# The last block's first layer as seven half-size products per 2x2 blocking, in an attention-plus-FFN kernel

## The chip, the cores and the metric

The kernel runs on one core of one Trainium2 chip. The metric is device time in microseconds, the median of the runs; lower is better. All times below are microseconds unless marked ns. The engines are PE (TensorE, matrix multiplications), DVE (VectorE), ACT (ScalarE), POOL (GpSimd) and SP (SyncE, which here only issues DMAs).

## The reference

```
# q, k, v: 8 batches, 8 heads, 576 positions, 64 wide; window of 64 positions
scores = q @ k^T / 8, masked to 0 <= pos_q - pos_k < 64
attn   = softmax(scores) @ v                  # per batch and head
x      = attn, heads side by side             # 4608 tokens x 512
h      = relu(x @ w_in)                       # w_in 512 x 2048
out    = (h * h) @ w_out                      # w_out 2048 x 512, out 4608 x 512 float32
```

The two multiplications with `w_in` and `w_out` are called layer 1 and layer 2.

## The kernel before

The 4608 tokens are worked on in nine blocks of 512: blocks 0 to 7 are the first 512 positions of each batch, and block 8 (called `B`) holds the last 64 positions of all eight. For each block there are the attention units (four pairs of heads: scores `Sc`, mask `M`, product with v `A`, transposition `X` into `xT`), layer 1 and layer 2.

*Layer 1* is `F1(g, f)`: for each of 16 slices of 128 of the 2048 hidden columns, four multiplications of 128x512 sum up in one PSUM bank (`hps`, L358). DVE takes the relu out of the bank (`hr`, L361), and ACT squares it into the 16-bit tile `h2` (L362). The banks of `hps` are two (`ps_f1`).

*Layer 2* of blocks 2 to 8 is already done with seven products in place of eight: `L2S(g, p, s, banks)` computes product p (1 to 7) of one half s of the token tiles, each as eight multiplications of 128x256 (`product`, L446). Two PSUM banks serve it, `chain` (256 columns of one bank) and `side` (two halves, `pa` and `pb`). For one s the products go in the order 1, 2, 6, 5, 7, 3, 4: products 1, 6, 7 and 4 add to one another in `chain`, and between them ACT copies the partial result out, scaled (`scaled`, L460), or DVE adds it to what is there (`plus`, L463). Product 1 starts a new sum in `chain`, so it must come after the copy made for the product that was in `chain` before. The sums of blocks of h that the products need are made by `S_sum` (DVE, L422, `hsum`), the sums of blocks of `w_out` once by `T_sum` (`wsum`).

All instructions are put in order by hand. The last loop goes over n = 1 to 8; the pass n is called phase n here. In phase n the layer 2 of block n and the layer 1 of block n + 1 alternate on PE. A string `order` of the digits 1 and 2 says in which order the groups of layer 1 and 2 follow, one group per digit; `put(i, work)` places other work ahead of group i: the attention units of block n + 2, the S sums, and DMA loads. Phase 7 has 16 groups of layer 1 of block 8 and 14 products of block 7, and no attention work. Phase 8 has only the 14 products of block 8; there the two halves s have banks of their own (`more`, which are the two `ps_f1` banks, and `chain` with `side`).

Each engine runs its own list in program order. An instruction that waits holds up all that stand behind it on its engine. PE's order in phase 7 is layer 1, layer 2, layer 1, ... ; ACT's list holds the squares of layer 1 and the scaled copies of layer 2, DVE's the relus, the adds of layer 2 and the S sums.

The attention tiles `at_ps[0]` and `at_ps[1]` (two PSUM banks each) are free in phase 7, since no attention is left. The pool `tpool` (five tiles with the tag T) holds the transposed q and k; `stp` (ten 128x512 32-bit tiles) holds loaded inputs.

Of the kernel before, what the change touches and what calls it, by code (L numbers as in the profile page):

```python
# [8 lines left out]
FP32 = mybir.dt.float32  # L9
FP16 = mybir.dt.float16  # L10
AF = mybir.ActivationFunctionType
ALU = mybir.AluOpType
# [3 lines left out]
def kernel(  # L16
# [13 lines left out]
    nc = tc.nc  # L30
# [3 lines left out]
    P = 128  # L34
    HP = H // 2
    NBLK = B + 1
    DMC = DM // P
    FFC = DFF // P
# [6 lines left out]
    stp = ctx.enter_context(tc.tile_pool(name="stp", bufs=10))  # L45
    p16p = ctx.enter_context(tc.tile_pool(name="p16p", bufs=6))
    vpool = ctx.enter_context(tc.tile_pool(name="vpool", bufs=2))
    tpool = ctx.enter_context(tc.tile_pool(name="tpool", bufs=5))
    apool = ctx.enter_context(tc.tile_pool(name="apool", bufs=2))
    xtpool = ctx.enter_context(tc.tile_pool(name="xtpool", bufs=2))  # L50
    h2pool = ctx.enter_context(tc.tile_pool(name="h2pool", bufs=2))
# [3 lines left out]
    ps_f1 = ctx.enter_context(tc.tile_pool(name="ps_f1", bufs=2, space=bass.MemoryType.PSUM))  # L55
# [47 lines left out]
    st = {}  # L103
# [12 lines left out]
    def copy(engine, out, in_):  # L116
        if engine is nc.scalar:
            engine.activation(out=out, in_=in_, func=AF.Copy, scale=1.0)  # L118
        else:
            engine.tensor_copy(out=out, in_=in_)  # L120


    w_in_sb = const.tile([P, DMC, DFF], FP16, name="w_in_sb")
# [121 lines left out]
    pm, av, xs, xT = {}, {}, {}, {}  # L245
    at_ps = [ps_at.tile([P, 2, 512], FP32, name=f"at{i}") for i in range(2)]
# [84 lines left out]
    def X(g, hp, engine=nc.scalar, pool=ps_tr, tag="tr", own=None):  # L331

        if g not in xT:
            xT[g] = xtpool.tile([P, DMC, 512], FP16, name="xT", tag="xT")
        if g == B:
            nc.sync.dma_start_transpose(out=xT[g][:, hp, :].rearrange("p (j t) -> p j t", j=4),
                                        in_=xs[g, hp][:].rearrange("p j h d -> p (j h d)"))
            return
        if own is not None:
            tr = at_ps[own][:, 0, :].bitcast(FP16).rearrange("p (a b) -> p a b", a=2)  # L340
        else:
            tr = pool.tile([P, 2, 512], FP16, name="xtr", tag=tag)
        for jp in range(4):
            nc.tensor.transpose(out=tr[:, 0, jp * P:(jp + 1) * P], in_=xs[g, hp][:, jp, :, :],  # L344
                                identity=ident[:])
        copy(engine, xT[g][:, hp, :], tr[:, 0, :])


    h2 = {}

    def F1(g, f, pool=ps_f1, tag="f1", into=None):
        if g not in h2:
            h2[g] = h2pool.tile([P, FFC, 512], FP16, name="h2", tag="h2")
        hps, done = open_f1.pop((g, f), (None, 0))
        if hps is None:
            hps = into if into is not None else pool.tile([P, 512], FP32, name="hps", tag=tag)
        for c in range(done, DMC):
            nc.tensor.matmul(hps[:], w_in_sb[:, c, f * P:(f + 1) * P], xT[g][:, c, :],  # L358
                             start=(c == 0), stop=(c == DMC - 1))
        hr = opool.tile([P, 512], FP32, name="hr", tag="hr")  # L360
        nc.vector.tensor_scalar(out=hr[:], in0=hps[:], scalar1=0.0, scalar2=None, op0=ALU.max)  # L361
        nc.scalar.activation(out=h2[g][:, f, :], in_=hr[:], func=AF.Square)  # L362
# [41 lines left out]
    HF = FFC // 2  # L404
# [6 lines left out]
    def a_of(g, i, j, s):  # L411
        t0 = 256 * i + 128 * s
        return h2[g][:, j * HF:(j + 1) * HF, t0:t0 + 128]
# [4 lines left out]
    def s_of(k, s):  # L418
        return S_sb[:, k - 1, :, 128 * s:128 * s + 128]

    def minus(out, a, b, op=ALU.subtract, engine=None):
        (engine or nc.vector).tensor_tensor(out=out, in0=a, in1=b, op=op)  # L422
# [11 lines left out]
    def S_sum(g, k, s):  # L434
        if k == 1:
            minus(s_of(1, s), a_of(g, 1, 0, s), a_of(g, 1, 1, s), ALU.add)
        elif k == 2:
            minus(s_of(2, s), s_of(1, s), a_of(g, 0, 0, s))
        elif k == 3:
            minus(s_of(3, s), a_of(g, 0, 0, s), a_of(g, 1, 0, s))  # L440
        else:
            minus(s_of(4, s), a_of(g, 0, 1, s), s_of(2, s))

    def product(to, a, b, start):
        for f in range(HF):
            nc.tensor.matmul(to, a[:, f, :], b[:, f, :], start=start and f == 0, stop=f == HF - 1,  # L446
                             skip_group_check=True)

    def flush():
        while to_store:  # L450
            to_store.pop(0)()
# [61 lines left out]
    seq = list(range(NBLK))  # L513
# [3 lines left out]
    with tc.manual_schedule():  # L517
# [21 lines left out]
        dve, pool, act = nc.vector, nc.gpsimd, nc.scalar  # L539
# [60 lines left out]
        three = [in_f1, in_f1, in_f2]  # L600
# [60 lines left out]
        first = iter([lambda f=f: F1(g1, f, into=at_ps[1][:, 1, :] if f == 2 else None) for f in range(FFC)])  # L661
# [5 lines left out]
        def A(g, hp, i=1):  # L667
            AV(g, hp, i)
            N(g, hp)
# [36 lines left out]
        done = 12  # L706
        chain = ps_f2.tile([P, 512], FP32, name="chain", tag="f2")
        side = ps_tr.tile([P, 512], FP32, name="side", tag="tr")
        for n in range(1, NBLK):
            g = seq[n]  # L710
            last = n == NBLK - 1
            one = None if last else seq[n + 1]
            if n == 1:
                second = [lambda ts=ts, i=i: F2(g, ts, i, None, None, into=(chain, side)[ts % 2])
                          for ts in range(4) for i in range(4)]
            elif last:
                more = [ps_f1.tile([P, 512], FP32, name="more", tag="f1") for _ in range(2)]
                banks = [(more[0][:, 0:HC], more[1]), (chain[:, 0:HC], side)]
                second = [lambda p=p, s=s: L2S(g, p, s, banks[s])
                          for p, s in ((1, 0), (2, 0), (1, 1), (6, 0), (2, 1), (5, 0), (7, 0),  # L720
                                       (6, 1), (3, 0), (4, 0), (5, 1), (7, 1), (3, 1), (4, 1))]
            else:
                second = [lambda p=p, s=s: L2S(g, p, s, (chain[:, 0:HC], side))
                          for s in range(2) for p in ORDER]
            first = [] if last else [lambda f=f: F1(one, f) for f in range(FFC)]
            order = ("22222222" + 8 * "112" if n == 1 else
                     "2" * 14 if last else
                     ("2112121212121211" if n == 2 else "1212121212121211") + "21212121121122")
            a, b = iter(first), iter(second)
            fill = [next(a if c == "1" else b) for c in order]  # L730
            at = {}

            def put(i, *work):
                at.setdefault(i, []).extend(work)

            if n == 1:
                put(0, lambda: Sc(g2, 3), lambda: A(g2, 2))
                put(2, lambda: M(g2, 3))
                put(3, lambda: X(g2, 2, own=1))
                put(5, lambda: A(g2, 3))  # L740
                put(7, lambda: X(g2, 3, own=1))
                for i, k in ((1, 1), (3, 2), (6, 3), (8, 4)):
                    put(i, lambda k=k: T_sum(k))
            else:
                for i, k, s in (((0, 1, 1), (0, 2, 1), (2, 4, 0), (3, 3, 1), (4, 4, 1)) if last else
                                ((2, 4, 0), (4, 1, 1), (6, 2, 1), (9, 3, 1), (18, 4, 1))):
                    put(i, lambda k=k, s=s: S_sum(g, k, s))
            if not last:
                end = len(fill) - 1
                put(24 if n == 1 else 20, lambda: S_sum(one, 3, 0))  # L750
                put(end if n == 1 else end - 1, lambda: S_sum(one, 1, 0))
                put(end, lambda: S_sum(one, 2, 0))
            base = 4 * (n + 2)
            for i, two in zip((11, 22) if n == 1 else (9, 20) if n == 2 else (9, 17) if n == 6 else (8, 19),
                              (units[base:base + 2], units[base + 2:base + 4])):
                for t, u in enumerate(two):
                    if u is not None:
                        put(i, lambda u=u, t=t: Sc(*u, i=t))
                        put(i + 3 + t, lambda u=u: M(*u))
                        put(i + 6, lambda u=u, t=t: A(*u, i=t))  # L760
                        put(i + (7 if u[0] == B else 8 + t), lambda u=u, t=t: X(*u, own=t))
            for i, group in enumerate(fill):
                for work in at.pop(i, []):
                    work()
                total = 12 + (30 * (n - 1) + i + 1) * (len(load_list) - 12) // 140
                while done < total and (parts_left or pending):
                    next_part()
                    done += 1
                group()
            assert not at, at.keys()  # L770
# [30 lines left out]
```

## Time and profile before

| what | us |
|---|---|
| median of 3 runs (297.67 to 298.23) | 298.13 |
| the profiled execution | 298.21 |
| its span, first to last instruction | 296.2 |
| phase 6 (223.90 to 253.63) | 29.73 |
| phase 7 (253.63 to 279.67) | 26.04 |
| phase 8 with the last stores (279.67 to 296.20) | 16.53 |

A phase is counted here from the start of its first group on PE to that of the next phase's first. The page of the profile gives the busy time of each engine and the chain of work that ended last; the timeline gives instructions in order of time, where "x8" means eight that follow one another, the second column is their length together, and a bracket at the end names an idle time ahead of them and what ended it. Matmuls overlap, so a burst of eight is written with 1.04 although the next one starts 0.87 after it.

### The profile page before, as it was taken

What the parts mean: (1) busy time and instruction counts of PE and PEld (TensorE: products, weight loads), DVE (VectorE), ACT (ScalarE), POOL (GpSimd) and SP (SyncE); (2) the same over time, 40 slices, a digit from 0 to 9 for tenths busy, and PEclk for the clock granted to TensorE, in tenths of its full rate; (3) what the DMA queues carried; (4) which work ended last, traced back from release to release, by engine and by line L of the source; (5) the groups of instructions that cost most, each with busy time, mean ns of one, the idle gap of its engine ahead of it and who ended that gap; (6) DMA issues with size and microseconds to landing.
All of it is one profiled execution on the core that took longest, in us unless ns stands there. A gap on an engine that the chain in (4) does not pass through costs nothing.

```text
span 296.2 us, 7372 instructions
## 1 busy us (share of the span) xinstructions
PE 287.7 (97%) x2905; PEld 180.3 (61%) x2905; DVE 216.3 (73%) x379; ACT 170.3 (57%) x292; POOL 125.8 (42%) x215
## 2 busy tenths in 40 slices
PE   7899999999999999999999999999999999999994
PEld 5543545555445466667666766676667666766783
DVE  4677539588867787878778877987788679866651
ACT  3666757688366656565665566556655654444521
POOL 4668848984383267229425633913232000000002
PEclk9999999999999999999999999999999999999999
DMA  6999999999999995999999999799997023100015
GB/s 209 259 323 392 407 326 237 321 247 196 177 254 185 190 216 106 209 181 234 181 207 226 200 180 226 157 198 200 196 221 202 2 38 107 73 37 35 2 71 142
DMA packets 143650, 56.05 MB, mean 189 GB/s; under 512 B 127712, under 2 KB 136160, under 8 KB 143616
## 3 DMA queue, kind: packets, MB, share of 16 engines
q1 hardware_dynamic: 143232, 55.00, 85.2%
q0 software_dynamic: 144, 0.39, 0.6%
q8 instruction: 22, 0.36, 0.5%
q10 hardware_dynamic: 240, 0.20, 0.3%
q14 instruction: 12, 0.10, 0.1%
HBM read 38.80 MB, written 9.44 MB: 163 GB/s over the span
## 4 chain that ended last, share of the span: by engine, by line
PE 88%; SPq 5%; DMA 4%; POOL 1%; ACT 0%; issue 0%; DVE 0%
PE hps L358 39%; PE chain L446 16%; PE side L446 12%; PE ops L394 5%; DMA wsum<-in_moe_w_in_dram 4%; PE at L318 4%; PE at L288 3%; PE side L394 2%; PE chain L394 2%; SPq L180 2%; PE more L446 2%; PE at L344 2%; SPq L173 2%; PE tr L257 1%; SPq L132 1%; SPq L139 1%
## 5 line engine op out<-in xcount | busy, mean ns | idle before, releaser
L362 ACT ACTIVATE h<-hr 128x512 f16<-128x512 f32 x144 | 90.2, 630 | 92.5 <-DVE hr L361 92.1
L358 PE MATMUL hps<-xT,w_in_sb 128*128 128x512 f16 x560 | 138.6, 379 | 0.5 <-POOL w_in_sb L120 0.4
L361 DVE TENSOR_SCALAR hr<-hps 128x512 f32<-128x512 f32 x143 | 97.2, 687 | 42.6 <-PE hps L358 39.4
L358 PEld LDWEIGHTS <-w_in_sb 128*128 128x128 f16 x564 | 52.8, 98 | 48.1 <-POOL w_in_sb L120 1.9
L446 PEld LDWEIGHTS <-hsum 128*128 128x128 f16 x448 | 43.2, 98 | 13.2
L120 POOL CAST v_ev<-st_v 128x512 f16<-128x512 f32 x31 | 21.6, 696 | 45.3 <-DMA st_v<-in_v_dram 45.3
L446 PEld LDWEIGHTS <-h 128*128 128x128 f16 x336 | 32.7, 98 | 9.3
L120 POOL CAST k<-st_k 128x512 f16<-128x512 f32 x33 | 21.4, 651 | 38.2 <-DMA st_k<-in_k_dram 30.4
L295 ACT ACTIVATE pm<-at 128x1024 f16<-128x1024 f32 x35 | 34.1, 1014 | 2.1 <-PE at L288 2.1
L387 POOL DMA_DIRECT2D out_dram<-osb x3 | 1.8, 595 | 63.6 <-ACT osb L460 62.2
L446 PE MATMUL chain<-wsum,hsum 128*128 128x256 f16 x208 | 27.0, 273 | 0.0
L328 DVE TENSOR_TENSOR xs<-at,rden 128x512 f16<-128x512 f32 x36 | 24.9, 692 | 1.2
L302 DVE TENSOR_TENSOR pm<-pm,mask 128x1024 f16<-128x1024 f16 x32 | 23.7, 754 | 1.9 <-ACT pm L295 1.9
L422 DVE TENSOR_TENSOR hsum<-h 128x1024 f16<-128x1024 f16 x28 | 20.4, 728 | 5.4 <-ACT h L362 5.4
L233 POOL CAST v_od<-st_v 64x512 f16<-64x512 f32 x30 | 22.4, 748 | 1.6
L120 POOL CAST q<-st_q 128x512 f16<-128x512 f32 x28 | 19.2, 711 | 4.7 <-DMA qT<-q 2.1
L394 PEld LDWEIGHTS <-h 128*128 128x128 f16 x128 | 11.6, 98 | 12.2
L460 ACT ACTIVATE osb<-chain 128x256 f32<-128x256 f32 x39 | 14.5, 373 | 5.6 <-PE chain L446 5.6
L318 PEld LDWEIGHTS <-pm 128*64 128x64 f16 x576 | 11.2, 110 | 6.9 <-DVE pm L302 3.2
L118 ACT ACTIVATE xT<-at 128x512 f16<-128x512 f16 x22 | 12.8, 587 | 4.0 <-PE at L344 4.0
L394 PE MATMUL ops<-w_out_sb,h 128*128 128x512 f16 x64 | 14.8, 380 | 0.0
L318 PE MATMUL at<-v_ev,pm 128*64 128x65 f16 x384 | 13.8, 197 | 0.2 <-ACT v_ev L118 0.2
(91 smaller groups left out, 317.2 us busy)
## 6 DMA issues: line engine op xcount, KB each, us to landing
st_k<-in_k_dram SPq DMA_DIRECT2D x37, 256.0 KB, 3.7
out_dram<-osb SPq DMA_DIRECT2D x32, 256.0 KB, 2.8
st_q<-in_q_dram SPq DMA_DIRECT2D x29, 256.0 KB, 4.9
st_v<-in_v_dram SPq DMA_DIRECT2D x28, 256.0 KB, 4.1
w_st<-in_moe_w_in_dram SPq DMA_DIRECT2D x4, 512.0 KB, 5.9
wsum<-in_moe_w_in_dram SPq DMA_DIRECT2D x4, 512.0 KB, 9.8
hsum<-in_moe_w_out_dram SPq DMA_DIRECT2D x4, 512.0 KB, 7.9
wsum<-in_moe_w_out_dram SPq DMA_DIRECT2D x4, 512.0 KB, 9.2
```

Source lines behind the costliest of these rows:

```text
L120: engine.tensor_copy(out=out, in_=in_)
L233: nc.gpsimd.tensor_copy(out=od[g][to:to + 64, m, :, 0:D], in_=st["v", g, c][of:of + 64, :].rearrange("p (h d) -> p h d", h=H))
L295: nc.scalar.activation(out=p[:, hh, :] if apart else p[:], in_=sc[hh] if apart else both[:], func=AF.Exp, scale=1.0 / float(D) ** 0.5)
L302: nc.vector.tensor_tensor(out=p[:], in0=p[:], in1=m.unsqueeze(1).broadcast_to([P, 2, 512]), op=ALU.min)
L318: nc.tensor.matmul(a[jj * 64:(jj + 1) * 64, hh, jp * VW:jp * VW + D + 1], pm[g, hp][:, hh, j * 64:(j + 1) * 64], vsel, start=True, stop=True)
L328: nc.vector.tensor_tensor(out=x[:].rearrange("p j h d -> p h j d"), in0=a[:, :, :, 0:D], in1=rden[:].unsqueeze(3).broadcast_to([P, 2, 4, D ...
L358: nc.tensor.matmul(hps[:], w_in_sb[:, c, f * P:(f + 1) * P], xT[g][:, c, :], start=(c == 0), stop=(c == DMC - 1))
L361: nc.vector.tensor_scalar(out=hr[:], in0=hps[:], scalar1=0.0, scalar2=None, op0=ALU.max)
L362: nc.scalar.activation(out=h2[g][:, f, :], in_=hr[:], func=AF.Square)
L394: nc.tensor.matmul(f2[g, ts][:], h2[g][:, f, ts * P:(ts + 1) * P], w_out_sb[:, f, :], start=(f == 0), stop=(f == FFC - 1))
L422: (engine or nc.vector).tensor_tensor(out=out, in0=a, in1=b, op=op)
L446: nc.tensor.matmul(to, a[:, f, :], b[:, f, :], start=start and f == 0, stop=f == HF - 1, skip_group_check=True)
```

## The change

Layer 1 of block 8, done in phase 7, is computed as a 2x2 block product with seven multiplications of blocks in place of eight. The blocks: the 512 inputs of `x` in halves k, the 512 tokens in halves j (256 each, `x_of(g, k, j)`), the 2048 hidden columns in halves i (`w_of(i, k)`). Product p has its own left and right operand, some of them sums: four sums of weight blocks (`W_sum`, tiles `wS` out of `tpool`) and four of x blocks (`X_sum`, tiles `xS`).

The hidden columns of a half are worked on in four pieces m of 256; `L1S(g, p, two, banks)` does product p for two pieces, each with four multiplications of 128x256. Three PSUM banks belong to a piece: a and b are banks of `at_ps`, c is a bank of `ps_f1`; so there are two sets of banks, one for m = 0 and 2, one for m = 1 and 3. The order of p is 5, 1, 2, 6, 7, 3, 4, first for m = 0, 1, then for m = 2, 3. Between products ACT copies partial sums from bank to bank (out of p = 5 into a kept tile, after 1 from a to b, after 6 from b to c, after 7 from c to a). The results come out with products 2, 7, 3 and 4: for 2 and 4 DVE takes the relu and ACT squares; for 7 and 3 DVE adds the kept product 5 first, and then, for m = 0 and 1, ACT does relu and square, while for m = 2 and 3 DVE does both in one operation. The squares on ACT are held in a list and issued one L1S step later, those of p = 4 at once.

Phase 7's order becomes "12" fourteen times. The weight sums are done on DVE in halves `cc` in phases 5, 6 and 7. Phase 8's products and S sums change their order: product (p, s) = (1, 1) comes ahead of (2, 0). The instruction lists of SP and POOL are the same as before.

```diff
+    def W_sum(k, engine, cc):
+        if k not in wsums:
+            t = tpool.tile([P, HP, 512], FP16, name="wS", tag="T")
+            wsums[k] = t[:].rearrange("p a b -> p (a b)").rearrange("p (c f) -> p c f", c=2)
+        a, b, op = {1: (w_of(1, 0), w_of(1, 1), ALU.add), 2: (wsums.get(1), w_of(0, 0), ALU.subtract),
+                    3: (w_of(0, 0), w_of(1, 0), ALU.subtract), 4: (w_of(0, 1), wsums.get(2), ALU.subtract)}[k]
+        cols = slice(cc * 512, cc * 512 + 512)
+        minus(wsums[k][:, :, cols], a[:, :, cols], b[:, :, cols], op, engine)
...
+    def product1(to, m, a, b, start):
+        for u in range(2):
+            f = (2 * m + u) * P
+            for cc in range(2):
+                nc.tensor.matmul(to[:, u * HX:(u + 1) * HX], a[:, cc, f:f + P], b[:, cc, :],
+                                 start=start and u == 0 and cc == 0, stop=cc == 1, skip_group_check=True)
...
+    def L1S(g, p, two, banks):
...
+        def square(m, i, j, hr):
+            squares.append(lambda: nc.scalar.activation(out=h_of(m, i, j), in_=wide(hr), func=AF.Square))
+
+        def done(m, i, j, bank):
+            hr = piece32("ls")
+            nc.vector.tensor_scalar(out=hr[:], in0=bank, scalar1=0.0, scalar2=None, op0=ALU.max)
+            square(m, i, j, hr)
+
+        def done5(m, i, j, bank):
+            y = piece32("ls")
+            nc.vector.scalar_tensor_tensor(out=y[:], in0=bank, scalar=1.0, in1=kept5[m][:],
+                                           op0=ALU.mult, op1=ALU.add)
+            if m < 2:
+                squares.append(lambda: nc.scalar.activation(out=y[:], in_=y[:], func=AF.Relu))
+                square(m, i, j, y)
+            else:
+                nc.vector.scalar_tensor_tensor(out=h_of(m, i, j), in0=wide(y), scalar=0.0, in1=wide(y),
+                                               op0=ALU.max, op1=ALU.mult)
+
+        held, squares[:] = list(squares), []
+        to, lhs, rhs, start = {5: (1, wsums.get(1), xsums.get(1), True), 1: (0, w_of(0, 0), x_of(g, 0, 0), True),
+                               2: (0, w_of(0, 1), x_of(g, 1, 0), False), 6: (1, wsums.get(2), xsums.get(2), False),
+                               7: (2, wsums.get(3), xsums.get(3), False), 3: (1, wsums.get(4), x_of(g, 1, 1), False),
+                               4: (0, w_of(1, 1), xsums.get(4), False)}[p]
+        for m in two:
+            product1(banks[m % 2][to], m, lhs, rhs, start)
+        for m in two:
+            a, b, c = banks[m % 2]
+            if p == 5:
+                kept5[m] = piece32("p5")
+                copy(nc.scalar, kept5[m][:], b)
+            elif p == 1:
+                copy(nc.scalar, b, a)
+            elif p == 2:
+                done(m, 0, 0, a)
+            elif p == 6:
+                copy(nc.scalar, c, b)
+            elif p == 7:
+                copy(nc.scalar, a, c)
+        for m in two:
+            a, b, c = banks[m % 2]
+            if p == 7:
+                done5(m, 1, 1, c)
+            elif p == 3:
+                done5(m, 0, 1, b)
+            elif p == 4:
+                done(m, 1, 0, a)
+        for f in held:
+            f()
+        if p == 4:
+            for f in squares:
+                f()
+            squares.clear()
...
-                          for p, s in ((1, 0), (2, 0), (1, 1), (6, 0), (2, 1), (5, 0), (7, 0),
+                          for p, s in ((1, 0), (1, 1), (2, 0), (6, 0), (2, 1), (5, 0), (7, 0),
                                        (6, 1), (3, 0), (4, 0), (5, 1), (7, 1), (3, 1), (4, 1))]
...
-            first = [] if last else [lambda f=f: F1(one, f) for f in range(FFC)]
+            apart = n == NBLK - 2
+            if apart:
+                cs = [ps_f1.tile([P, 512], FP32, name="c", tag="f1") for _ in range(2)]
+                three = [(at_ps[0][:, i, :], at_ps[1][:, i, :], cs[i][:]) for i in range(2)]
+                first = [lambda p=p, two=two: L1S(one, p, two, three)
+                         for two in ((0, 1), (2, 3)) for p in (5, 1, 2, 6, 7, 3, 4)]
+            else:
+                first = [] if last else [lambda f=f: F1(one, f) for f in range(FFC)]
...
+                     "12" * 14 if apart else
...
-                for i, k, s in (((0, 1, 1), (0, 2, 1), (2, 4, 0), (3, 3, 1), (4, 4, 1)) if last else
+                for i, k, s in (((1, 3, 0), (2, 1, 1), (3, 2, 1), (4, 4, 0), (6, 3, 1), (8, 4, 1)) if last else
+                                ((2, 4, 0), (4, 1, 1), (6, 2, 1), (12, 3, 1), (19, 4, 1)) if apart else
...
+            for i, k, cc in {NBLK - 4: ((19, 1, 0), (22, 1, 1)),
+                             NBLK - 3: ((2, 2, 0), (9, 2, 1), (17, 3, 0), (26, 3, 1)),
+                             NBLK - 2: ((3, 4, 0), (17, 4, 1))}.get(n, ()):
+                put(i, lambda k=k, cc=cc: W_sum(k, dve, cc))
+            if n == NBLK - 3:
+                put(25, lambda: X_sum(seq[-1], 1))
+            if apart:
+                for i, k in ((0, 2), (2, 3), (4, 4)):
+                    put(i, lambda k=k: X_sum(one, k))
```

The two halves of a slot of `L1S` are its two pieces m. In the text that follows, a slot is one group of eight 128x256 multiplications of phase 7, counted from 0: even slots are steps of `L1S`, odd slots products of `L2S`.

More of the change, by code (lines that the diff above doesn't have):

```diff
@@ L447, in product, with w_of, x_of @@
                              skip_group_check=True)
+    wsums, xsums = {}, {}
+    HX = 256
+    def w_of(i, k):
+        return w_in_sb[:, 2 * k:2 * k + 2, i * HF * P:(i + 1) * HF * P]
+    def x_of(g, k, j):
+        return xT[g][:, 2 * k:2 * k + 2, j * HX:(j + 1) * HX]
+    def W_sum(k, engine, cc):
[6 more added lines that the diff above has]
+        minus(wsums[k][:, :, cols], a[:, :, cols], b[:, :, cols], op, engine)
@@ new lines, in X_sum @@
+    def X_sum(g, k):
+        if k not in xsums:
+            t = apool.tile([P, 2, 512], FP16, name="xS", tag="pm", bufs=4)
+            xsums[k] = t[:, 0, :].rearrange("p (c t) -> p c t", c=2)
+        a, b = {1: (x_of(g, 0, 1), x_of(g, 0, 0)), 2: (x_of(g, 1, 1), xsums.get(1)),
+                3: (x_of(g, 1, 1), x_of(g, 0, 1)), 4: (x_of(g, 1, 0), xsums.get(2))}[k]
+        minus(xsums[k], a, b)
+    def product1(to, m, a, b, start):
[4 more added lines that the diff above has]
+                                 start=start and u == 0 and cc == 0, stop=cc == 1, skip_group_check=True)
@@ new lines, with h_of, wide, piece32 @@
+    kept5 = {}
+    squares = []
+    def L1S(g, p, two, banks):
+        if g not in h2:
+            h2[g] = h2pool.tile([P, FFC, 512], FP16, name="h2", tag="h2")
+        def h_of(m, i, j):
+            return h2[g][:, i * HF + 2 * m:i * HF + 2 * m + 2, j * HX:(j + 1) * HX]
+        def wide(t):
+            return t[:].rearrange("p (u t) -> p u t", u=2)
+        def piece32(name):
+            return stp.tile([P, 512], FP32, name=name, tag="st")
+        def square(m, i, j, hr):
[48 more added lines that the diff above has]
+            squares.clear()
@@ L749 @@
                 end = len(fill) - 1
-                put(24 if n == 1 else 20, lambda: S_sum(one, 3, 0))
-                put(end if n == 1 else end - 1, lambda: S_sum(one, 1, 0))
+                if not apart:
+                    put(24 if n == 1 else 20, lambda: S_sum(one, 3, 0))
+                put(end if n == 1 or apart else end - 1, lambda: S_sum(one, 1, 0))
                 put(end, lambda: S_sum(one, 2, 0))
```

## The prediction

> **What bounds the kernel now.** I read the page first: its engine table and the shares of the chain that ended last. Times are microseconds, widths are partitions x elements.
>
> ```profile
> span 296.2 us, 7372 instructions
> PE 287.7 (97%) x2905; PEld 180.3 (61%) x2905; DVE 216.3 (73%) x379; ACT 170.3 (57%) x292; POOL 125.8 (42%) x215
> PE 88%; SPq 5%; DMA 4%; POOL 1%; ACT 0%; issue 0%; DVE 0%
> ```
>
> TensorE sets the end; VectorE (DVE) and ScalarE (ACT) are hardly on the chain. Then the busy times by phase, for phases 6, 7 and 8 (the pass n = 6, 7, 8 of the last loop):
>
> ```profile
> 223.90:253.63 29.73, 29.73 (x315) 19.86 (x312) 23.61 (x43) 16.86 (x31) 1.27 (x2) 1.00 0.26 74
> 253.63:279.67 26.04, 26.04 (x179) 17.24 (x176) 18.05 (x31) 12.37 (x24) 0.00 (x0) 1.00 0.11 42
> 279.67:296.20 16.53, 12.39 (x114) 10.86 (x111) 7.00 (x14) 3.46 (x9) 1.78 (x3) 1.00 0.34 95
> ```
>
> After the length come PE, PEld, DVE, ACT, POOL, then the granted clock. In phase 7 PE is busy for all 26.04; DVE has 8.0 and ACT 13.7 to spare. The timeline of PE shows what one slot of its work costs:
>
> ```profile
> 251.88 1.04 PE L446 MATMUL side<-w_out_sb,hsum 128*128 128x256 f16 x8
> 252.76 1.04 PE L446 MATMUL chain<-wsum,h 128*128 128x256 f16 x8
> 253.63 1.03 PE L358 MATMUL hps<-xT,w_in_sb 128*128 128x512 f16 x4
> 254.49 1.04 PE L446 MATMUL chain<-w_out_sb,h 128*128 128x256 f16 x8
> ```
>
> From start to start eight 256-wide multiplications take 0.87 (0.873 as a mean over phase 8: 14 of them from 279.67 to 291.89), four 512-wide 0.86. The second burst ends at 252.76 + 1.04 = 253.80, and the copy that reads it starts at 253.83 (first line of the next fence). So a reader starts 1.07 after a slot's start, and a reader of its first half, four of eight, at 0.44 + 0.20 = 0.64. ACT's and DVE's spacing when they have a backlog:
>
> ```profile
> 253.83 0.38 ACT L460 ACTIVATE osb<-chain 128x256 f32<-128x256 f32 x1 [0.32 <-PE chain L446]
> ...
> 193.22 0.63 ACT L362 ACTIVATE h<-hr 128x512 f16<-128x512 f32 x1 [1.98 <-DVE hr L361]
> 193.75 0.58 ACT L118 ACTIVATE xT<-at 128x512 f16<-128x512 f16 x1
> ...
> 94.21 0.59 ACT L398 ACTIVATE osb<-chain 128x512 f32<-128x512 f32 x1
> 94.69 0.60 ACT L118 ACTIVATE xT<-at 128x512 f16<-128x512 f16 x1
> ...
> 212.43 0.38 ACT L460 ACTIVATE osb<-chain 128x256 f32<-128x256 f32 x1
> 212.69 0.60 ACT L118 ACTIVATE xT<-at 128x512 f16<-128x512 f16 x1
> ```
>
> ```profile
> 195.49 0.42 DVE L463 SCALAR_TENSOR_TENSOR osb<-side,osb 128x256 f32<-128x256 f32 x1
> 195.83 0.68 DVE L422 TENSOR_TENSOR hsum<-hsum,h 128x1024 f16<-128x1024 f16 x1
> 196.43 0.69 DVE L361 TENSOR_SCALAR hr<-hps 128x512 f32<-128x512 f32 x1
> 197.03 0.68 DVE L422 TENSOR_TENSOR hsum<-h,hsum 128x1024 f16<-128x1024 f16 x1
> ...
> 208.41 0.21 DVE L325 RECIPROCAL rden<-at 128x8 f32<-128x8 f32 x1 [0.16 <-PE at L318]
> 208.65 0.69 DVE L328 TENSOR_TENSOR xs<-at,rden 128x512 f16<-128x512 f32 x1
> ```
>
> Operations overlap their neighbours, so a queue moves by the spacing: on ACT 0.53 for a 512-wide Square from SBUF, 0.48 for a 512-wide copy from PSUM, 0.27 for a 256-wide one; on DVE 0.60 for a 512-wide relu or a 1024-wide 16-bit sum, 0.34 for a 256-wide add. An operation that needs its predecessor's result waits for its end plus 0.03 (208.41 + 0.21 to 208.65).
>
> **The change part by part.** *Multiplications.* Phase 7 loses 64 of 512 columns and gains 112 of 256, that is 14 new slots of eight. It becomes 28 slots: 28 x 0.873 = 24.44 against 26.04, **-1.60**. The weight loads double in number but at 98 ns stay under the 109 ns spacing, as L446's do already.
>
> *Sums.* Eight weight sums (1024-wide 16-bit, 0.60 each) and four sums of x (512-wide, at most 0.60) go to DVE in phases 5, 6 and 7. SP's and POOL's lists stay the same and no DMA is added or moved. The cover is DVE's idle time (6.1 in phase 6, 8.0 in phase 7) and the time before a bank is written again: in phase 6 the relu at 227.71 is put back to 228.31 by the sum ahead of it and ends at 229.00; its bank is next written at 229.97. The two sums that take a tile over from qT wait for the score multiplications placed with them; these end 0.1 before DVE gets there in phase 5, and in an idle stretch in phase 6. I cost them at 0; without cover each would be worth up to 0.60. In phase 7 X_sum(2), S_sum, X_sum(3), the weight sum and X_sum(4) fill DVE to t = 4.9 (t runs from the phase's start) and put back the first relu, whose bank isn't needed before t = 8.2: 0 too.
>
> *The first wait.* Each L1S product issues its ACT copies and then the squares held from the step before. From slot 6 (5.24 + 0.64 = 5.88) ACT never idles in the first half (m = 0, 1): two copies c<-b 0.96, two squares 1.06, a scaled copy 0.27, two copies a<-c 0.96, then for steps 7 and 3 four pairs of a Relu and the Square that needs it, each 0.63 + 0.03 + 0.53 = 1.19, together 4.76, then two squares of step 4, 1.06. That ends at 5.88 + 9.07 = 14.95. Only then comes the scaled copy out of `chain` for block 7's product 4 (slot 13): it ends at 14.95 + 0.37 + 0.03 = 15.35. Slot 15 starts a new sum in `chain` and needs it; its own turn is 15 x 0.873 = 13.10. Behind it on PE stands everything. **+2.25**. Bounds: if the Square doesn't wait for its Relu and the copies go at half the spacing of the 1024-wide Exp (0.45), 1.6; if nothing overlaps (0.63 and 0.59 each; no row shows a copy from PSUM into PSUM), 3.5. I take the backlog rows, which these operations match in width and source.
>
> [...]
>
> *The second wait.* In the second half (m = 2, 3) DVE squares steps 7 and 3 itself: `done5` (0.69 + 0.03) and an operation on its result (0.60), 1.32 a pair. From slot 22 + 0.64 its list is four pairs 5.28, two adds 0.68, two relus of step 4, 0.60 + 0.69: 7.25. ACT's list has both squares of step 4 ahead of the scaled copy out of `chain` (slot 27), so that copy comes 0.03 + 0.53 + 0.37 + 0.03 = 0.96 after the second relu: 8.85 after the start of slot 22. Phase 8's second product, (1, 1), now starts `chain`: by the count it stands 7 slots after slot 22, at 6.11. **+2.74**. What it would otherwise do next, (2, 0), needs the same squares. Bounds: no wait inside a pair 2.26; if the 32-bit square from SBUF, which has no row, ran at 0.30 (half of L422's 1024-wide 16-bit sum), 1.1; with no overlap 3.3. I take 0.60, the row of 512 elements of 32 bits.
>
> The first wait gives the second nothing: both ends of the latter move with slot 22. The other S sums of phase 8 end before their products.
>
> Sum: -1.60 + 2.25 + 2.74 = **+3.4**, on the profiled execution's 298.21 (span 296.2 and 2.0 around it) 301.6; the median of the runs, 298.13, is 0.1 lower: **301.5**.
>
> **The rivals.** *Both queues keep up* (the other side): the shorter multiplications count in full, 298.1 - 1.6 = 296.5. The place is the scaled copy out of `chain`. ACT would have to do its 9.47 from slot 6 in 7.2, near 0.41 per 512-wide operation, and DVE with ACT behind it 8.21 in 5.47; the change stops being slower where the two waits together fall under 1.6. For it: the idle shares of phase 7; 16-bit sums run at 0.30 per 512. Against it: no 32-bit row is under 0.48.
>
> *One wait only*: if the pairs on ACT go faster than I think, the second wait alone leaves 298.1 - 1.6 + 2.7 = 299.3 (with its low price 297.6); if the 32-bit squares on DVE are short, the first with the rest of the second, 298.1 - 1.6 + 2.25 + 1.1 = 299.9. For it: no row prices a Relu in place. Against it: two queues have to be judged, each on rows of its own.
>
> *The waits slow the clock.* The granted clock is 1.00 in all phases, and PE's longest wait in this trace is 1.4, so a gap of 2.3 to 2.7 isn't tried here. If four slots after a wait ran at half rate it would be 4 x 0.87 = 3.5 more, 305.0 for one such wait. [...]
>
> *It doesn't do what it says*: if the weight sums hold DVE up after all, at most eight times 0.60 on top, 306; the relu slack above speaks against it.
>
> **How the numbers follow.** Both waits 0.75; one wait 0.12; both queues keep up 0.08; clock 0.03; weight sums 0.02. The range is that of the first two: low bounds 298.1 - 1.6 + 1.6 + 1.1 = 299.2, high 298.1 - 1.6 + 3.5 + 3.3 = 303.3; I give 299.0 to 303.4. About 0.2% (0.6) is what a measurement of this kernel can tell from no change. Faster: the 0.08 and 0.01 of one wait at its low price. Same: 0.05, from one wait priced low. Slower: the rest, 0.86.
>
> **What would show it.** Phase 7's slots of 0.87 with no gap up to slot 14; then a PE gap of about 2.2 before `chain<-w_out_sb,h` of slot 15, while ACT runs Relu and Square back to back; no gap in slots 16 to 27; a gap of about 2.7 after the first product of phase 8, while DVE works without idle and ACT waits for it; phases 5 and 6 as long as before. Wrong: no PE gap at slot 15, a clock under 1.00, or longer phases 5 and 6.

## The result, and the profile after

The changed kernel takes 307.47 (median of 6 runs, 305.26 to 308.93) where the kernel before took 298.54 beside it (6 runs): a ratio of 1.0282, 95% interval 1.0224 to 1.0341. It is slower, as forecast, but by 9 and not by 3.4. The page of its profiled execution, which took 305.26:

```profile
span 303.5 us, 7514 instructions
PE 287.3 (95%) x2953; PEld 185.2 (61%) x2953; DVE 224.4 (74%) x395; ACT 177.9 (59%) x308; POOL 126.3 (42%) x215
PE 82%; ACT 6%; DVE 6%; issue 3%; DMA 2%; SPq 1%; DVEq 0%; ACTq 0%
```

ACT and DVE have 6% each of the chain that ended last, where they had none. The busy times by phase (columns as before) say where:

```profile
253.65:283.59 29.94, 25.23 (x226) 21.85 (x224) 18.42 (x34) 19.14 (x38) 0.00 (x0) 1.00 0.10 36
283.59:303.50 19.91, 12.55 (x114) 10.85 (x111) 10.66 (x20) 4.45 (x11) 1.78 (x3) 1.00 0.29 80
```

Phase 7 begins at 253.65, where it began at 253.63. That isn't yet a sign that the sums in phases 5 and 6 cost nothing: phase 5 began 0.66 earlier in this execution (194.34 against 195.00), and e1 comes back to it. Phase 7 takes 29.94 in place of 26.04, with PE busy for only 25.23; phase 8 takes 19.91 in place of 16.53. PE's timeline, start, length, instruction, and in brackets an idle time and what ended it:

```profile
256.27 1.04 PE L446 MATMUL side<-w_out_sb,h 128*128 128x256 f16 x8
257.77 1.03 PE L480 MATMUL at<-xT,w_in_sb 128*128 128x256 f16 x8 [0.47 <-ACT at L118]
...
259.52 1.04 PE L480 MATMUL at<-xS,wS 128*128 128x256 f16 x8
...
266.57 1.04 PE L480 MATMUL at<-xS,wS 128*128 128x256 f16 x8
270.55 1.03 PE L446 MATMUL chain<-w_out_sb,h 128*128 128x256 f16 x8 [2.94 <-ACT osb L565]
...
277.31 1.09 PE L480 MATMUL c<-xS,wS 128*128 128x256 f16 x8
...
280.86 1.04 PE L480 MATMUL at<-xS,w_in_sb 128*128 128x256 f16 x8
282.72 1.03 PE L446 MATMUL chain<-wsum,h 128*128 128x256 f16 x8 [0.83 <-DVE osb L568]
283.59 1.04 PE L446 MATMUL more<-w_out_sb,h 128*128 128x256 f16 x8
287.84 1.03 PE L446 MATMUL chain<-w_out_sb,h 128*128 128x256 f16 x8 [3.21 <-ACT osb L565]
```

A burst's turn is 0.87 after the start of the one ahead of it; what is over is a gap. Slot 6 is the line at 259.52, slot 22 that at 277.31. So slot 4 comes 0.63 late (257.77 against 257.14), slot 15 3.11, slot 27 0.99, and phase 8's second product 3.38; slot 18 is 0.63 late again. ScalarE between, first up to slot 15, then in phase 8:

```profile
256.53 1.20 ACT L118 ACTIVATE at<-at 128x512 f32<-128x512 f32 x2 [0.39 <-PE at L480]
...
260.65 1.07 ACT L118 ACTIVATE c<-at 128x512 f32<-128x512 f32 x2 [0.55 <-PE at L480]
...
262.92 1.22 ACT L118 ACTIVATE at<-c 128x512 f32<-128x512 f32 x2
264.36 0.63 ACT L513 ACTIVATE ls<-ls 128x512 f32<-128x512 f32 x1 [0.21 <-DVE ls L510]
265.02 0.63 ACT L501 ACTIVATE h<-ls 128x512 f16<-128x512 f32 x1
265.56 0.61 ACT L513 ACTIVATE ls<-ls 128x512 f32<-128x512 f32 x1
...
268.56 1.67 ACT L501 ACTIVATE h<-ls 128x512 f16<-128x512 f32 x3
270.14 0.36 ACT L565 ACTIVATE osb<-chain 128x256 f32<-128x256 f32 x1
...
278.95 1.22 ACT L118 ACTIVATE at<-c 128x512 f32<-128x512 f32 x2
286.29 1.23 ACT L501 ACTIVATE h<-ls 128x512 f16<-128x512 f32 x2 [6.11 <-DVE ls L505]
287.42 0.36 ACT L565 ACTIVATE osb<-chain 128x256 f32<-128x256 f32 x1
```

Both times the short copy out of `chain` (L565) is the last of a row, and PE's next burst into `chain` starts 0.05 to 0.06 after its end. In the second row ACT had idled 6.11 for VectorE's relu of product 4. VectorE's work ahead of that:

```profile
279.59 0.69 DVE L510 SCALAR_TENSOR_TENSOR ls<-c,p 128x512 f32<-128x512 f32 x1 [2.76 <-ACT at L118]
280.32 0.69 DVE L516 SCALAR_TENSOR_TENSOR h<-ls 128x512 f16<-128x512 f32 x1
...
285.57 1.28 DVE L505 TENSOR_SCALAR ls<-at 128x512 f32<-128x512 f32 x2
```

It is one unbroken list from 279.59 on, but it starts 2.28 after slot 22 (277.31), when ScalarE has made the first of its two copies out of banks c (from 278.95 on).

A measure without the early phases, whose lengths vary: from the start of slot 0 to the start of PE's last burst it is 291.02 - 253.63 = 37.39 before and 298.31 - 253.65 = 44.66 after, +7.27. This is called the stretch below.

### The profile page after: what moved, and what is told of

Same layout as the page of the kernel before. It is cut to its first block, busy times and chain, and to the rows that moved or that the text cites. A ratio compares the mean times of both kernels' runs of the same rounds, so it can differ in the third digit from the quotient of the medians.

```text
span 303.5 us, 7514 instructions
## 1 busy us (share of the span) xinstructions
PE 287.3 (95%) x2953; PEld 185.2 (61%) x2953; DVE 224.4 (74%) x395; ACT 177.9 (59%) x308; POOL 126.3 (42%) x215
## 4 chain that ended last, share of the span: by engine, by line
PE 82%; ACT 6%; DVE 6%; issue 3%; DMA 2%; SPq 1%; DVEq 0%; ACTq 0%
PE hps L358 34%; PE chain L446 14%; PE side L446 9%; PE ops L394 5%; PE at L318 3%; PE at L288 3%; PE side L394 2%; PE chain L394 2%; PE at L480 2%; DMA st_k<-in_k_dram 2%; PE more L446 2%; PE at L344 2%; DVE pm L302 1%; PE tr L257 1%; ACT h L501 1%
## 5 line engine op out<-in xcount | busy, mean ns | idle before, releaser
L362 ACT ACTIVATE h<-hr 128x512 f16<-128x512 f32 x128 | 80.1, 630 | 79.2 <-DVE hr L361 79.0
L358 PE MATMUL hps<-xT,w_in_sb 128*128 128x512 f16 x496 | 122.4, 379 | 0.3 <-DVE hr L361 0.2
L361 DVE TENSOR_SCALAR hr<-hps 128x512 f32<-128x512 f32 x127 | 85.8, 686 | 32.1 <-PE hps L358 28.8
L358 PEld LDWEIGHTS <-w_in_sb 128*128 128x128 f16 x500 | 46.8, 98 | 42.6 <-issue 1.7
L120 POOL CAST v_ev<-st_v 128x512 f16<-128x512 f32 x31 | 23.1, 744 | 43.1 <-DMA st_v<-in_v_dram 43.1
L565 ACT ACTIVATE osb<-chain 128x256 f32<-128x256 f32 x39 | 14.6, 373 | 8.9 <-PE chain L446 8.8
L446 PE MATMUL chain<-w_out_sb,h 128*128 128x256 f16 x104 | 13.5, 272 | 6.1 <-ACT osb L565 6.1
L568 DVE SCALAR_TENSOR_TENSOR osb<-side,osb 128x256 f32<-128x256 f32 x26 | 10.9, 418 | 6.1 <-ACT at L118 4.6
```

## The experiments

The kernel before, run beside them, had medians from 298.18 to 298.37. The output of e6 and e8 is off by a relative 0.175; that of e9, which only adds two multiplications into the two banks c ahead of slot 0, is that of the reference. The author read this as product 7 not adding, in e6 and e8, to what ScalarE copied into bank c, so that this part of the sum is missing in their h; no trace shows it. PE, ACT and DVE run the same operations.

| run | median us | stretch in the profile | gaps over 0.3 |
|---|---|---|---|
| before | 298.2 to 298.5 | 37.39 | none |
| changed | 307.47; e12: 307.40 | 44.66; e12: 46.15 | 0.63, 3.11, 0.63, 0.99, 3.38 |
| e1 sums only | 298.56 | 37.39 | none |
| e2 sets | 304.54 | 43.73 | 0.53, 0.54, 1.66, 1.93, 0.88 |
| e3 alternate | 306.44 | 45.24 | 0.64, 0.36, 0.32, 2.93, 0.64, 2.65 |
| e4, e13 dummies | 305.61, 305.62 | 44.67, 44.69 | as changed, filled |
| e5 late squares | 304.04 | 42.42 | 0.63, 2.08, 0.77, 1.00, 1.19, 0.37, 0.44 |
| e6 four edits | 297.0 | 35.96 | none |
| e7 swap | 306.11 | 44.36 | 0.64, 2.80, 0.63, 2.78 |
| e8 no alternation | 300.47 | 39.08 | 1.60, 0.66, 0.37, 0.45 |
| e9 primed | 297.37 | 35.96 | none |
| e10 all, other banks | 300.16 | 38.55 | 0.52, 0.35, 0.85, 0.32 |
| e11 three edits | 298.66 | 37.69 | 0.63, 0.98 |

Gaps are counted at full clock; where the clock was halved (e2, e3, e7, e12), the stretch holds 1.5 to 1.7 more.

**e1, the sums alone.** To the kernel before, `W_sum` and `X_sum` with their `put` lines are added, and nothing reads them.

> The kernel before with only the twelve sums of weights and of x added on VectorE (their results are not used). Theory A (the loss lies in phases 7 and 8, in waits of the new layer 1): 298 to 298.5, no phase longer by more than 0.1, granted clock 1.00. Theory B (the sums hold VectorE up): 1 us or more above the kernel before.

298.56, ratio 1.0004 (0.9986 to 1.0023), the stretch unchanged to the hundredth. Theory B, 1 or more, falls, but the sums aren't quite free. From the start of phase 5 (its first group on layer 1) to slot 0 the profile before has 58.63 (195.00 to 253.63) and e1's 59.04 (195.19 to 254.23); the other 13 profiles with the sums have 58.94 to 59.31 (e9's to its two extra multiplications). (Phase 6 itself starts at 224.76 before: the 223.90 used ahead of the prediction lies in the last product of phase 5.) The profile shows where, VectorE and PE before, then in e1:

```profile
217.44 1.70 DVE L302 TENSOR_TENSOR pm<-pm,mask 128x1024 f16<-128x1024 f16 x2
219.57 0.26 PE L318 MATMUL at<-v_ev,pm 128*64 128x65 f16 x5
```

```profile
217.63 0.68 DVE L302 TENSOR_TENSOR pm<-pm,mask 128x1024 f16<-128x1024 f16 x1
218.23 1.10 DVE L422 TENSOR_TENSOR wS<-w_in_sb 128x1024 f16<-128x1024 f16 x1
219.25 0.68 DVE L302 TENSOR_TENSOR pm<-pm,mask 128x1024 f16<-128x1024 f16 x1
219.77 0.47 PE L318 MATMUL at<-v_ev,pm 128*64 128x65 f16 x5
```

Half of a weight sum stands between two masks, and PE's product with v takes 0.21 longer while it waits for the second one. The other 0.20 is in the first layer 1 group of phase 6 (1.06 to the next start, where it was 0.86). The median of e1 can't tell these 0.4 from nothing, and no run moves the half sum to test this reading.

**e2, the banks by sets.**

```diff
-three = [(at_ps[0][:, i, :], at_ps[1][:, i, :], cs[i][:]) for i in range(2)]
+three = [(at_ps[i][:, 0, :], at_ps[i][:, 1, :], cs[i][:]) for i in range(2)]
```

> The changed kernel, only that each of the two sets takes its banks a and b from one attention tile of its own, in place of a from one tile and b from the other. Theory A (waits go by whole tiles, so that piece m = 0 waits for m = 1's copies too): the gaps of 0.63 ahead of slots 4 and 18 are gone, ScalarE starts its copies about 0.4 earlier and without 0.6 between the two of a step, the gap at slot 15 falls from 3.1 to about 2.5; in all some 2 us less, 303 in a run at clock 1.00. Theory B (a copy from PSUM into PSUM is slow by itself, or PE and ScalarE collide in the banks): the gaps at slots 4 and 18 stay, 305 to 308 as the changed kernel.

304.54, ratio 1.0209 (1.0177 to 1.0242). The gaps of slots 4 and 18 are gone and the one at slot 15 is 1.66. New ones of about 0.5 stand where a product into b waits for a read of a (slot 6), or one into a for a read of b (slot 12), now in the same tile. So an attention tile is waited for as a whole. Nor is a copy between banks slow by itself: the two copies of product 1 take 1.07 together here (257.05), with two target tiles, and 1.20 in the changed kernel, with one. In the second half the wait for VectorE's list moves to slot 26 (1.93 and 0.88, product 4 into a), with half the clock behind it (0.59 and 0.55 in the two stretches of 2 us from 284). At full clock the stretch would be some 2.6 shorter than the changed kernel's, where 2 was expected. The median is still 1.5 above the expected 303: two of the four runs had mean clocks of 0.991 and 0.992, and in the profiled one slot 0 came 0.95 later.

**e3, the pairs of relu and square divided evenly.**

```diff
-            if m < 2:
+            if m % 2 == 0:
```

> The changed kernel, only that ScalarE does relu and square of products 7 and 3 for m = 0 and 2 and VectorE for m = 1 and 3, in place of ScalarE for 0 and 1 and VectorE for 2 and 3. Theory A (two queues, each overloaded in one half): ScalarE has two pairs of 1.19 less ahead of the copy out of chain, so that the gap at slot 15 falls from 3.1 to about 0.7; VectorE has two squares of 0.6 less in the second half, so that the gaps at slot 27 and in phase 8 (4.4 together) fall to about 3.2; 301.5 to 302 at clock 1.00. Theory B (the number of operations or of bank changes sets the time, wherever they are done): no change, 305 to 308.

306.44, ratio 1.028 (1.0241 to 1.0318). The expectation was missed: the gap at slot 15 is 2.93. ScalarE just ahead of it:

```profile
268.27 0.63 ACT L501 ACTIVATE h<-ls 128x512 f16<-128x512 f32 x1
270.47 1.23 ACT L501 ACTIVATE h<-ls 128x512 f16<-128x512 f32 x2 [1.56 <-DVE ls L505]
271.60 0.37 ACT L565 ACTIVATE osb<-chain 128x256 f32<-128x256 f32 x1
```

ACT is free by 268.9 and then waits 1.56 for VectorE, which now has more to do, to reach product 4's relu; the copy out of `chain` stands behind the two squares that need this relu. At this gap it is the place in the list that costs, not ACT's load alone. All gaps of this run add up to 7.8, with 0.29 at slot 27, where the changed kernel has 8.8: the even division alone is worth 0.9, and not the 3.6 expected.

**e5, the squares of product 4 one step later.**

```diff
-        if p == 4:
-            for f in squares:
-                f()
-            squares.clear()
...
+            if last:
+                put(0, *squares)
+                squares.clear()
```

> The changed kernel, only that the squares of product 4 aren't issued at once but one step later, as those of the other products are (in the second half after the copy out of chain for block 7's last product). Theory A (the copy out of chain stands behind squares in ScalarE's list): two squares, 1.06, leave the queue ahead of the copy, the gap at slot 15 falls from 3.1 to 2.05; in phase 8 the second product goes in its turn and the gap moves to the third, (2, 0), which needs the squares themselves: about 2.2 in place of 3.4. In all 2.3 less, 303 at clock 1.00. Theory B (what PE waits for in phase 8 is VectorE's list, however ScalarE's is ordered): only the first gap changes, 304.2.

304.04, ratio 1.0198 (1.0165 to 1.0231). PE shows the first gap cut by the 1.06 of two squares and the last one moved to (2, 0):

```profile
270.86 1.03 PE L446 MATMUL chain<-w_out_sb,h 128*128 128x256 f16 x8 [1.90 <-ACT osb L561]
...
287.41 0.39 PE L446 MATMUL more<-w_out_sb,h 128*128 128x256 f16 x2 [1.03 <-ACT h L501]
288.00 0.39 PE L446 MATMUL more<-w_out_sb,h 128*128 128x256 f16 x2 [0.20 <-ACT h L501]
```

2.08 at slot 15, and 1.19 + 0.37 + 0.44 = 2.00 in phase 8. The stretch is 2.24 shorter, where 2.3 was expected; the median is 1 above the expected 303. In the profiled run (304.34) slot 0 came 1.34 later than in the changed kernel's (254.99 against 253.65), which accounts for it there; the other runs have no trace.

**e7, VectorE's addition ahead of ScalarE's copy of bank c.** The two branches for p == 7, `copy(nc.scalar, a, c)` and `done5(m, 1, 1, c)`, change places.

> The changed kernel, only that for product 7 VectorE's addition out of bank c stands ahead of ScalarE's copy of that bank in the list. Theory A (two engines that read one bank are ordered as the list has them, so VectorE's four pairs of the second half start only after ScalarE's copy): VectorE starts them about 1.1 earlier, the gaps at slot 27 and in phase 8 fall from 4.4 together to about 3.3; the gap at slot 15 stays at 3.1; 304.2 at clock 1.00. Theory B (the addition waits for product 5's copy or for PE): no change, 305.3 or more.

306.11, ratio 1.0261 (1.0221 to 1.0301). VectorE's first addition out of c in the second half, then PE's slot 22 and the burst behind the gap in phase 8:

```profile
279.03 0.69 DVE L510 SCALAR_TENSOR_TENSOR ls<-c,p 128x512 f32<-128x512 f32 x1 [1.17 <-ACT c L118]
```

```profile
278.33 1.09 PE L480 MATMUL c<-xS,wS 128*128 128x256 f16 x8
...
287.27 1.87 PE L446 MATMUL chain<-w_out_sb,h 128*128 128x256 f16 x8 [2.61 <-ACT osb L565]
```

The addition starts 0.70 after slot 22 in place of 2.28, the gap at slot 27 is gone and the one in phase 8 is 2.78: together 1.6 less, as much as VectorE gained. Slot 15's, which was expected to stay at 3.11, fell to 2.80, since the additions of the first half come earlier too and ScalarE's relus no longer wait 0.21 for them. Behind the gap in phase 8 a burst of eight takes 1.87 in place of 1.04, at half clock (0.50 from 288 to 290). All four runs had mean clocks of 0.988 to 0.994, as five of the six of the changed kernel had, and the median is 1.4 below its 307.47. So the order of the list decided when VectorE read bank c, 2.28 after slot 22 behind the copy and 0.70 ahead of it; here the order given cost 1.6.

**e6 and e8, the edits together.** The edits of e3, e5 and e7, and the banks as `(at_ps[i][:, 0, :], cs[i][:], at_ps[i][:, 1, :])`; e8 leaves out the alternation of e3.

> Four edits of the changed kernel together: the squares of product 4 one step later; ScalarE takes the pairs of m = 0 and 2 and VectorE those of m = 1 and 3; product 7's VectorE addition stands ahead of ScalarE's copy of the same bank; banks a and c of a set lie in one attention tile of its own and b in a bank by itself. Theory A (the loss is made of waits of the two lists): no gap at slots 4 and 18, under 0.5 at slot 15, about 1.0 ahead of (2, 0) in phase 8; -1.6 + 1.0 to 1.5 against the kernel before, 298 (297 to 299), clock 1.00. Theory B (the new operations are too many for the two engines in phase 7, whatever their order): gaps of 3 us or more in all stay, 301 or more.

> As e6_all but with the pairs divided as in the changed kernel (ScalarE for m = 0 and 1, VectorE for 2 and 3). Theory A: no gap at slots 4 and 18; about 1.3 at slot 15 (3.1 less 1.06 for the squares and 0.7 for the earlier start and the copies that overlap); about 2.1 to 2.5 in phase 8, where VectorE's 7.25 of work still ends late; 300 to 300.5 at clock 1.00, so that the even division of e6_all is worth about 2. Theory B (the order of the list is all): as e6_all within 0.5.

e6: 297.0, ratio 0.9971 (0.995 to 0.9993), no gap at all, not even the 1.0 that was expected in phase 8. e8: 300.47, ratio 1.0073 (1.0049 to 1.0098), 1.60 at slot 15 and 1.5 in phase 8, where 1.3 and 2.1 to 2.5 were expected. So the even division, worth 0.9 alone, is worth 39.08 - 35.96 = 3.1 beside the other three edits.

**e9, e10, e11, with the whole layer computed.** e9 is e6 with two multiplications ahead of slot 0:

```diff
+                for i in range(2):
+                    nc.tensor.matmul(at_ps[i][:, 1, :], ident[:], w_out_sb[:, 0, :], start=True, stop=True)
```

Why a write by PE ahead of ScalarE's copy makes the difference, these runs don't show. e10 has the banks of e2, e11 those of the changed kernel.

> As e6_all, in which product 7 didn't add to what ScalarE had copied into bank c (the bank, in an attention tile, had not been written whole by PE before, so the part of products 1, 2 and 6 was missing there); here two multiplications of 128x512 (0.43 us) write the two banks c ahead of slot 0, so that the whole layer is computed. Theory A (the seven products are worth 1.6 and cost nothing once the two lists are in a good order): 297.0 + 0.4 = 297.4 where the kernel before has 298.2, no gap on PE in phases 7 and 8. Theory B (e6_all was fast because part of the sum was left out): 299 or more.

> As e6_all, but the banks a and b of a set lie in one attention tile and c in a bank by itself (the assignment of e2_sets), with the whole layer computed. Theory A (waits go by whole tiles): product 6 into b waits for VectorE's read of a, product 3 into b for the copy into a, product 4 into a for the addition out of b, each some 0.4 to 0.5 in each half, about 2.4 in all: 299.4. Theory B (only real dependencies count): 297.0 as e6_all.

> As e6_all, but with the banks as the changed kernel has them (a of both sets in one attention tile, b of both in the other, c in banks by themselves), with the whole layer computed. Theory A: the gaps of 0.63 ahead of slots 4 and 18 are back and the copies of a step start after both pieces, 0.5 later, so that the slots behind the copy out of chain wait a few tenths: 297.0 + 1.3 to 2.0 = 298.3 to 299.0. Theory B (the order of the list is all): 297.0.

e9: 297.37, ratio 0.9978 (0.9958 to 0.9998). Its PE around the two old gaps:

```profile
253.74 0.59 PE L831 MATMUL at<-w_out_sb,ident 128*128 128x512 f16 x2
254.18 1.04 PE L480 MATMUL c<-xS,wS 128*128 128x256 f16 x8
...
266.40 1.04 PE L480 MATMUL c<-xS,wS 128*128 128x256 f16 x8
267.28 1.04 PE L446 MATMUL chain<-w_out_sb,h 128*128 128x256 f16 x8
...
278.75 1.04 PE L446 MATMUL more<-w_out_sb,h 128*128 128x256 f16 x8
279.62 1.04 PE L446 MATMUL chain<-w_out_sb,h 128*128 128x256 f16 x8
```

(The tile called c holds banks b in this run.) Slot 15 and phase 8's second product follow in their turn, 0.88 and 0.87 behind. The stretch is 37.39 - 35.96 = 1.43 below that of the kernel before, less 0.44 for the priming; the median is 0.9 below the 298.26 beside it. e10: 300.16 with gaps of 0.3 to 0.85 at products into b; e11: 298.66, ratio 1.0008 (0.9988 to 1.0028), with gaps of 0.63 and 0.98 at slots 4 and 18. e9 and e11 came out as expected. e10 is 0.8 above the 299.4 expected: its stretch is 2.6 longer than e6's, where 2.4 was expected, and slot 0 came 1.0 later than e6's in the profiled run. Which banks share a tile is worth 1.7 to 2.6.

**e4, e13 and e12, the clock.** Multiplications that nobody reads fill the two long gaps; e12 is the changed kernel again, on the same chip as e13.

```diff
+                if apart and i == 15:
+                    warm_up(side, 26)
+                if last and i == 1:
+                    warm_up(more[1], 30)
```

> The changed kernel with multiplications that nobody reads put where PE waits: 26 of 128x256 ahead of slot 15 (2.84 us) and 30 ahead of phase 8's second product (3.28 us), into banks that are free there. Theory A (gaps of about 3 us lower the granted clock in most runs, and this makes the runs of the changed kernel scatter from 305.3 to 308.9): the clock is 1.000 in every run and the median falls to about 305.3, with a scatter like that of the kernel before. Theory B (the scatter has another source): the median stays at 307.5 and the runs scatter as before, or rises by what the dummies cost.

> The changed kernel itself, beside e13 on the same chip. Theory A (after a PE gap of 2.8 us and more the granted clock is halved for some 3.4 us in most runs, which makes up the 2.2 between the profiled 305.3 and the median 307.5): median 307 to 308, scatter 3 us or more; in the profile either no stretch below clock 1.00 and a time of about 305.3, or one or two stretches at 0.5 right behind the gaps at slot 15 and in phase 8, each worth 1.7 more. Theory B (the scatter has another source): the time doesn't go with the clock.

> The changed kernel with multiplications that nobody reads in its two long gaps, as e4_dummy, beside e12 on the same chip. Theory A: 305.3 to 305.8 median, about 2 below e12, no stretch below clock 1.00 in phases 7 and 8. Theory B: the same as e12 within 0.5.

e4: 305.61 (304.98 to 306.54); e13: 305.62 (304.48 to 306.19); e12: 307.40 (305.92 to 309.04). The dummies cost nothing (stretch 44.69) and take 1.8 off the median. The granted clock behind the gap at slot 15 in e12's profile, which took 307.46 (it stands after POOL's busy time):

```profile
270.00:272.00 2.00, 0.71 (x5) 0.56 (x5) 0.00 (x0) 2.00 (x5) 0.00 (x0) 0.88 0.00 0
272.00:274.00 2.00, 2.00 (x11) 1.42 (x10) 0.00 (x0) 0.60 (x2) 0.00 (x0) 0.50 0.35 131
274.00:276.00 2.00, 1.74 (x12) 1.22 (x10) 0.17 (x1) 1.16 (x2) 0.00 (x0) 0.76 0.00 0
```

0.24 + 1.00 + 0.48 = 1.7 lost, where the same gap in the first profile of the changed kernel (305.26) went by at 1.00. The other five runs behind its median of 307.47 had mean clocks of 0.988 or 0.994 and took 306.8 to 308.9.

## Why the prediction was right in direction and wrong in size

- *The multiplications, -1.60*: right. The slots follow at 0.87, and with no gaps (e6) the stretch is 1.43 shorter.
- *The sums, 0*: nearly right. They cost 0.4 in phases 5 and 6 (e1; 0.68 in the first profile of the changed kernel). The prediction looked for cover at the relus and at the tiles taken over; the mask that PE waits for wasn't in its count.
- *The first wait, +2.25*: the place and the cause were right, down to the pairs (1.18 to 1.20 against 1.19). It measured 3.11. The step that failed is that "a reader of its first half" starts at 0.64: product 6 fills banks b, which lie in one tile, and ScalarE's copies began 1.13 after slot 6 (260.65 against 259.52), 0.49 late. The rest, 0.4, is the copies from c into a, which by their common target followed each other at 0.61 and not 0.48, and the short wait for VectorE behind them.
- *The second wait, +2.74*: mechanism right, the length of the list too (from 279.59 to PE's start at 287.84 it is 8.25, against 8.21). Mis-sized was its start: "from slot 22 + 0.64" was 2.28, since the addition out of c waited for ScalarE's copy of c. With that the wait measured 0.99 (slot 27) + 3.38 = 4.37, 1.63 more; e7 gave 1.6 of it back.
- *No gap up to slot 14 nor from 16 to 27*: wrong. PE waits for both pieces' copies at slots 4 and 18, 2 x 0.63; the prediction let each piece wait for its own. e2 and e11 against e6 show it.
- Together: 3.4 + 0.86 + 1.63 + 1.26 = 7.1, against +7.27 in the stretch. The 7.05 between the profiled executions is close to it because the 0.68 in phases 5 and 6 happens to meet an earlier start of phase 5 by 0.66.
- *The waits slow the clock*, given 0.03: this holds in most runs (a mean clock of 0.988 or 0.994 in five of the six) and adds most of the 2.2 between 305.26 and 307.47 (with the gaps filled, 1.8 of it goes). So two of the prediction's own signs of being wrong came: a clock under 1.00, and phases 5 and 6 slightly longer. Its price of 3.5 for one wait was too high; it was 1.7 (e12). No run shows the four slots at half rate that this price takes: where the clock fell to 0.50 (e3, e7, e12), two or three bursts ran slower and 1.5 to 1.7 was lost.
- *The weight sums, rival*: 0.4 and not eight times 0.60 (e1). *Both queues keep up*: not so in the changed kernel; e6 and e9 keep up with the same operations, ordered and divided otherwise, at 297.0 and 297.4 where the prediction had 296.5.

## What to carry to other kernels

When work is moved to idle engines, look at the order of each list and not at the idle share: here one 0.36 copy that PE needs stood behind up to twelve operations that nobody needed soon. Here waits went by tile (which banks share one was worth 1.7 to 2.6: e11 and e10 against e6) and by the order in which engines read a bank (1.6: e7), so give pieces that should run apart tiles of their own, and let the engine with the longer list read first. A gap of PE near 3 us can cost its own length and, behind it, half the clock for some bursts (0.50 in e12), here 1.7 more; an edit worth 0.9 alone (e3) was worth 3.1 beside the others.

## What was not expected of the hardware

The granted clock fell to 0.50 behind gaps of 2.78 (e7), 2.65 (e3) and 3.11 (e12), and in e2 behind two gaps of 1.93 and 0.88 with four multiplications between (0.59 and 0.55 in the two stretches of 2 us that follow). It stayed at 1.00 behind 3.11 and 3.38 in the first profile, behind 3.37 in e12, and at slot 15 behind 2.80 (e7) and 2.93 (e3), so the length alone doesn't decide; what else does, these runs leave open.
